# Second stage of a two-stage transformer kernel: order of projections and output columns in the first and the last batch

## The chip, the cores and the metric

The kernel runs on one core of a Trainium2 chip. The metric is the device time of one execution in microseconds (us). A core has five engines that the text names as the profile does: PE (matmuls; PEld is its weight load), DVE (vector), ACT (scalar, which also does the activations), POOL (general purpose) and SP, whose queue (SPq) issues the DMA transfers.

## The reference, cut to what matters

Three stages run one behind the other on 8 batches of 576 tokens and 512 features: a pooled attention, a gated MLP, and a block of four causal attention experts of which each token uses two. Only the last one is touched by the change:

```python
def _moe2_ref(x, w_gate, wq, wk, wv, wo):       # x: 8 x 576 x 512, E = 4 experts, Hd = 64
    logits = x @ w_gate
    topk = np.argpartition(-logits, K, axis=-1)[..., :K]
    ...                                          # w: softmax over the two chosen logits
    for e in range(E):
        q, k, v = x @ wq[e], x @ wk[e], x @ wv[e]
        scores = scale * (q @ k.transpose(0, 2, 1))
        scores = np.where(causal, -1000000000.0, scores)
        a = exp(scores - rowmax); a /= a.sum(-1, keepdims=True) + 1e-09
        ye = a @ v @ wo[e]
        ...                                      # out += w[:, e] * ye where e is chosen
    return out
```

## The kernel before, in words

The class PhaseA computes the first two stages for all batches and leaves their result in DRAM as a high and a low half (a product of two such numbers is taken as three matmuls, high times high, low times high, high times low). The class PhaseB is the experts' stage, and it is what the change touches. The hand-over from PhaseA to PhaseB lies at about 589 us of the span.

PhaseB cuts a batch into two pairs of experts (p = 0, 1) and each pair into nine *units* (table `QT`, L612): unit 0 holds the last 64 queries of both experts, units 1 to 4 are the other four blocks of 128 queries of the first expert from the longest to the shortest, units 5 to 8 those of the second. A unit has three steps:

- `score` (L816): two to six matmuls into PSUM, on DVE the mask with the row maximum (L832, L834, L841), on ACT the exponential with the row sum (L844) into one of five buffers `pr`.
- `scale` (L847): on DVE 1 over the sum (L853 or L855, L856), and the multiplication of the row by it and by the expert's gate (L860). That multiplication runs on POOL, except for the units listed in `SDF` (first batch) and `SDL` (last batch), where it runs on DVE.
- `trans` (L862): transposes on PE (L873, L886), a high half on ACT (L877, L890), a low half on DVE (L882, L891).

Behind unit 5 and unit 8 of a pair follows `av` (L893), the product with v of one expert (PE L906, ACT L910, DVE L911); the second expert's `av` also makes `ah` and `al`, the high and low half of the pair's result (L916 ACT, L917 DVE). They come from four buffers of the tag "x2", so the tiles of one batch can be written only when the output columns of the batch before have read theirs.

Between the units lie the projections, named by short codes. `10` to `13` are q half 0, q half 1, k half 0 and k half 1 of the batch's second pair; `00` to `03` the same of the next batch's first pair; each is 12 matmuls of `proj` (L705, matmuls L713 to L715). Behind q come copies on ACT and subtractions on DVE (L726 to L734) and, after half 1, two DMAs into the tiles `qz` (L737), which the units 1 to 8 need. Behind k come L744 on ACT, L745 on DVE and, after half 1, four DMAs into `kd` (L751). `v0` to `v4` are the v projections (L756: 12 matmuls each, 8 for `v4`), whose last four columns are the gate's logits; `g` is the gate (L789: 13 small DVE steps and one exponential, L796 to L812). `x0` to `x3` load the next batch's input (L634, three DMAs each); its low half `xbl` has a single buffer, so it can be loaded only when all projections of the batch at hand are done. `o0` to `o3` are the output columns of the batch before (`outp`, L919: for each of two query ranges six matmuls, three per pair, then ACT L931; one DMA, L932).

`run` (L934) issues first the list `PRE` (L621) for batch 0, then unit by unit: `score` of unit k, `scale` of unit k-1, the codes that `FIRSTF` (batch 0), `FILL` or `LASTF` (batch 7) list for the unit, `av` where it is due, `trans` of unit k-3. The last batch's own columns come at the end (L977). The framework orders each engine's instructions ahead of the run: by the program's order, but an instruction whose inputs it reckons to be late is overtaken by later ones of the same engine. On the chip each engine then runs its list in order. PSUM has 8 banks, which all tiles of PhaseB share (L702).

Of the kernel before, what the change touches and what calls it, by code (L numbers as in the profile page):

```python
# [8 lines left out]
F32 = mybir.dt.float32  # L9
# [7 lines left out]
B, H, S, D = 8, 8, 576, 64  # L17
# [596 lines left out]
ALV = 1  # L614
KDM = 1
FILL = (('', '12 10 11', '', '13 x0 x1 x2 x3', '', '', 'o3 o1 o0', '', ''), ('v0', 'v1 00 02', '01 o2', '03', '', '', '', 'v2 v3', 'v4 g'))
FIRSTF = (('10', '11', '12', '13 x0 x1 x2 x3', '', '', '', '', ''), ('v0 00', '', '01 02 v1', '03', '', '', '', 'v2 v3', 'v4 g'))
LASTF = (('', '10 12 11', '', '', '13', '', 'o1', '', 'o0'), ('', '', '', '', '', 'o2', '', '', 'o3'))
SDF = {(0, 0), (0, 1), (0, 5), (0, 8), (1, 0), (1, 2), (1, 7)}
SDL = {(0, 4), (0, 6), (1, 6), (1, 7)}  # L620
PRE = 'v0 00 01 02 03 v1 v2 v3 v4 g'  # L621
AVS = [(0, 256), (256, S)]


class PhaseB:


    def __init__(self, ctx, tc, w, ins, x2d, out, ident):
        self.tc, self.nc, self.ins, self.x2d, self.out, self.ident = tc, tc.nc, ins, x2d, out, ident
        self.c = self.w = w  # L630
        self.ps = ctx.enter_context(tc.tile_pool(name="b_ps", bufs=1, space=bass.MemoryType.PSUM))
        self.X, self.QK, self.V, self.GW, self.U, self.PT, self.AV, self.AH = {}, {}, {}, {}, {}, {}, {}, {}

    def load_x(self, b, kc):  # L634
        nc, w = self.nc, self.w
# [211 lines left out]
    def scale(self, b, p, u):  # L847
# [6 lines left out]
        else:  # L854
# [3 lines left out]
        n = min(S, 128 * i + 128)  # L858
        (nc.vector if (p, u) in (SDF if b == 0 else SDL if b + 1 == B else ()) else
         nc.gpsimd).tensor_scalar(pt[:, :n], pt[:, :n], st[:, 3:4], g, op0=OP.mult, op1=OP.mult)  # L860
# [55 lines left out]
            nc.scalar.activation(ah[:, lo:up], a[:, lo:up], AF.Copy)  # L916
            (nc.vector if ALV else nc.gpsimd).tensor_sub(al[:, lo:up], a[:, lo:up], ah[:, lo:up].bitcast(F32))  # L917

    def outp(self, b, f):  # L919
        nc, w = self.nc, self.w  # L920
        c = slice(128 * f, 128 * f + 128)
        o = w.tile([128, S], F32, tag="vg", name="o", bufs=3)
        for lo, up in AVS:
            ps = self.bank("op")[:, :up - lo]
            s = slice(lo, up)
            for p in range(2):
                ah, al = self.AH[b, p]
                nc.tensor.matmul(ps, self.wo[0][:, p, c], ah[:, s], start=p == 0, stop=False)
                nc.tensor.matmul(ps, self.wo[1][:, p, c], ah[:, s], start=False, stop=False)
                nc.tensor.matmul(ps, self.wo[0][:, p, c], al[:, s], start=False, stop=p == 1)  # L930
            nc.scalar.activation(o[:, s], ps, AF.Copy)  # L931
        nc.sync.dma_start(self.out[b, :, f], o)  # L932

    def run(self):  # L934
        self.consts()
        for kc in range(4):
            self.load_x(0, kc)
        self.weights()
        part = lambda b, p: [lambda w=w, h=h: self.proj(b, w, p, h) for w in "qk" for h in range(2)]
        vpart = lambda b: [lambda t=t: self.vproj(b, t) for t in range(NT)]  # L940
        units = [(b, p, u) for b in range(B) for p in range(2) for u in range(9)]
        def item(b, x):
            if x[0] == "x":
                return [lambda: self.load_x(b + 1, int(x[1]))] if b + 1 < B else []
            if x[0] == "o":
                return [lambda: self.outp(b - 1, int(x[1]))] if b > 0 else []
            if x[0] == "1":
                return [part(b, 1)[int(x[1])]]
            if b + 1 == B:
                return []  # L950
            if x[0] == "0":
                return [part(b + 1, 0)[int(x[1])]]
            if x[0] == "v":
                return [vpart(b + 1)[int(x[1])]]
            return [lambda: self.gate(b + 1)]
        for x in PRE.split():
            for f in item(0 if x[0] == "1" else -1, x):
                f()
        for k in range(len(units) + LAG + 1):
            if k < len(units):  # L960
                b, p, u = units[k]
                self.score(b, p, u)
            if 0 <= k - 1 < len(units):
                self.scale(*units[k - 1])
            if k < len(units):
                for x in (LASTF if b + 1 == B else FILL if b else FIRSTF)[p][u].split():
                    for f in item(b, x):
                        f()
            j = k - LAG
            if 0 <= j - 1 < len(units):  # L970
                b_, p_, u_ = units[j - 1]
                if u_ in (5, 8):
                    for g in range(2):
                        self.av(b_, p_, u_ // 8, g)
            if 0 <= j < len(units):
                self.trans(*units[j])
        for f in range(4):  # L977
            self.outp(B - 1, f)


def host_b(inputs, a):
# [34 lines left out]
```

## Time and profile before

| | us |
|---|---|
| median of 3 runs | 968.05 (966.70 to 968.46) |
| the profiled execution | 967.84 |
| its span, first to last instruction | 966.1 |
| PE busy in the span | 915.0 (95%) |
| DVE, ACT, POOL busy | 693.1, 519.0, 447.0 |

The span is what the traces show; the execution's own time is 1.74 us longer than it. A group of instructions is shown with its line, engine, operation, output and inputs. Start times are counted from the span's start. Matmuls overlap, so the length of one is not what it costs; the distance of starts is. A row of busy time by stretch gives the stretch, its length, then the busy us (with the number of instructions) of PE, PEld, DVE, ACT and POOL, the granted clock of PE as a share of 2.4 GHz, the DMA share and GB/s. A row in order of time gives start, length, engine, line and operation, and in brackets the idle time before it with what ended it.

### The profile page before, as it was taken

The page shows a single profiled execution, that of the slowest core. Times are in us where ns is not written, and L with a number is a line of the kernel's source. Part 1 is how long each engine was busy: PE and PEld are TensorE (multiplying, and loading weights), DVE is VectorE, ACT ScalarE, POOL GpSimd, SP SyncE. Part 2 cuts the span into 40 slices and gives each one's busy share as a digit, 9 for nine tenths or more (in the row PEclk, how much of TensorE's full clock was granted, in tenths as well). Part 3 has the DMA queues.
Part 4 walks back from the last instruction along what each step waited for, and adds up shares of the span by engine and source line. Part 5 has one row for each costly group of instructions (what it writes and reads, how often), then busy time and mean ns, then how long its engine had stood idle before and what let it go on. Part 6 is the DMA issues. An engine that isn't in the chain of part 4 may idle for free.

```text
span 966.1 us, 18451 instructions
## 1 busy us (share of the span) xinstructions
PE 915.0 (95%) x6488; PEld 864.4 (89%) x6488; DVE 693.1 (72%) x1869; ACT 519.0 (54%) x1285; POOL 447.0 (46%) x628
## 2 busy tenths in 40 slices
PE   4887699999999999999999999899999999999997
PEld 3677689989989999899899899799999999999987
DVE  6998557757667577577576514897878796878785
ACT  3755334344343343343443433677777777777776
POOL 6545847558369368376583560113222222323221
PEclk9797899999999999999999999999999999999999
DMA  9611522312402404223126014415253534435121
GB/s 326 236 35 44 172 80 82 121 61 71 157 25 81 160 13 140 99 65 132 56 61 191 25 39 134 140 37 176 61 172 88 162 94 147 118 108 163 49 61 75
DMA packets 51644, 102.86 MB, mean 106 GB/s; under 512 B 10592, under 2 KB 16736, under 8 KB 50656
## 3 DMA queue, kind: packets, MB, share of 16 engines
q1 hardware_dynamic: 51408, 101.68, 32.9%
q8 instruction: 52, 0.85, 0.4%
q14 instruction: 40, 0.33, 0.1%
q10 hardware_dynamic: 144, 0.00, 0.0%
HBM read 59.72 MB, written 28.31 MB: 91 GB/s over the span
## 4 chain that ended last, share of the span: by engine, by line
PE 63%; DVE 20%; ACT 6%; POOL 5%; issue 3%; DMA 2%; SPq 1%; POOLq 0%; ACTq 0%; DVEq 0%
PE av L906 4%; PE op L457 4%; PE op L458 4%; PE op L459 3%; PE sp L434 3%; PE sp L432 3%; PE sp L433 3%; PE sc L224 3%; PE t L886 3%; DVE vnl L402 3%; PE pj L715 2%; PE pj L713 2%; PE pj L714 2%; DVE vnh L404 2%; DVE bs L388 2%
## 5 line engine op out<-in xcount | busy, mean ns | idle before, releaser
L860 POOL TENSOR_SCALAR pr<-pr,sm,gw 128x128 f32<-128x128 f32 (+3 forms) x119 | 72.7, 612 | 208.1 <-DVE sm L856 140.9
L844 ACT ACTIVATE pr<-s,sm 128x256 f32<-128x256 f32 (+4 forms) x160 | 83.2, 521 | 41.6 <-DVE sm L841 18.0
L432 PE MATMUL sp<-wsh,vnh 128*128 128x288 f32 x256 | 78.8, 309 | 5.0 <-ACT vnh L400 5.0
L458 PE MATMUL op<-g,woh 128*128 128x288 f32 x256 | 77.0, 301 | 6.8 <-POOL g L445 6.8
L457 PE MATMUL op<-g,woh 128*128 128x288 f32 x256 | 78.5, 309 | 0.3 <-DVE x2l L464 0.3
L416 PE MATMUL up<-x,wih 128*128 128x288 f32 x256 | 76.8, 300 | 1.5 <-ACT xu L324 1.5
L433 PE MATMUL sp<-wsh,vnl 128*128 128x288 f32 x256 | 77.0, 301 | 0.0
L434 PE MATMUL sp<-wsl,vnh 128*128 128x288 f32 x256 | 76.6, 299 | 0.0
L418 PE MATMUL up<-x,wil 128*128 128x288 f32 x256 | 75.7, 296 | 0.0
L715 PE MATMUL pj<-xbh,wql 128*128 128x288 f32 x256 | 75.5, 295 | 0.0
L713 PE MATMUL pj<-xbh,wqh 128*128 128x288 f32 x256 | 75.5, 295 | 0.0
L714 PE MATMUL pj<-xbl,wqh 128*128 128x288 f32 x256 | 75.5, 295 | 0.0
L459 PE MATMUL op<-g,wol 128*128 128x288 f32 x256 | 75.3, 299 | 0.0
L417 PE MATMUL up<-x,wih 128*128 128x288 f32 x256 | 75.1, 293 | 0.0
L841 DVE CUSTOM_DVE_ANT_0 s<-s,mk 128x512 f32<-128x512 f32 (+3 forms) x128 | 62.4, 487 | 3.5 <-PE t L886 2.9
L224 PE MATMUL sc<-kbd,qt 128*128 128x144 f32 (+1 forms) x320 | 50.8, 306 | 14.2 <-DMA qt<-q_in 8.4
L891 DVE TENSOR_TENSOR pbl<-t,pbh 128x512 fp32r<-128x512 f32 (+3 forms) x128 | 60.7, 484 | 3.4 <-ACT pbh L890 1.7
L886 PE MATMUL t<-ident,pr 128*128 128x128 f32 x320 | 57.7, 280 | 4.8 <-POOL pr L860 2.6
L224 PEld LDWEIGHTS sc<-kbd,qt 128*128 128x128 f32 (+1 forms) x320 | 44.4, 192 | 18.3 <-issue 11.1
L906 PE MATMUL av<-pbh,vt 128*128 128x320 f32 (+4 forms) x224 | 55.6, 278 | 2.4 <-ACT pbh L890 2.4
L400 ACT ACTIVATE vnh<-vg,rs 128x512 fp32r<-128x512 f32 (+1 forms) x40 | 27.3, 717 | 54.9 <-POOL rs L392 43.0
L464 POOL TENSOR_TENSOR x2l<-x2l,x2h 128x576 fp32r<-128x576 f32 x8 | 11.4, 1430 | 97.1 <-ACT x2h L463 97.1
(247 smaller groups left out, 3352.8 us busy)
## 6 DMA issues: line engine op xcount, KB each, us to landing
kraw<-k_in SPq DMA_DIRECT2D x16, 576.0 KB, 3.8
x<-x2h SPq DMA_DIRECT2D x32, 288.0 KB, 2.1
x<-x2l SPq DMA_DIRECT2D x32, 288.0 KB, 2.1
xbl<-x SPq DMA_DIRECT2D x32, 288.0 KB, 4.1
xbh<-x SPq DMA_DIRECT2D x32, 288.0 KB, 4.0
kd<-scr SPq DMA_DIRECT2D x64, 144.0 KB, 2.5
out<-o SPq DMA_DIRECT2D x32, 288.0 KB, 3.7
vraw<-v_in SPq DMA_DIRECT2D x16, 512.0 KB, 4.3
```

What stands on the lines that cost most here:

```text
L224: nc.tensor.matmul(ps[:m, p // 2, (p % 2) * 144:(p % 2) * 144 + 144], qt[:, p, o:o + m], kbd[:, p, :], start=p % 2 == 0, stop=True, skip_g ...
L432: nc.tensor.matmul(o, vh[:, k, c], self.ws[0][:, k, s], start=k == 0, stop=False)
L433: nc.tensor.matmul(o, vl[:, k, c], self.ws[0][:, k, s], start=False, stop=False)
L434: nc.tensor.matmul(o, vh[:, k, c], self.ws[1][:, k, s], start=False, stop=False)
L457: nc.tensor.matmul(o, self.wo[0][:, k, c], gh[:, s], start=k == 0, stop=False)
L458: nc.tensor.matmul(o, self.wo[0][:, k, c], gl[:, s], start=False, stop=False)
L459: nc.tensor.matmul(o, self.wo[1][:, k, c], gh[:, s], start=False, stop=k == 3)
L713: nc.tensor.matmul(ps, self.wq[0][:, kc, c], xh[:, s], start=kc == 0, stop=False)
L714: nc.tensor.matmul(ps, self.wq[0][:, kc, c], xl[:, s], start=False, stop=False)
L715: nc.tensor.matmul(ps, self.wq[1][:, kc, c], xh[:, s], start=False, stop=kc == 3)
L886: nc.tensor.transpose(ps[:, j], pt[:, 128 * j:128 * j + 128], self.ident)
L906: nc.tensor.matmul(ps[:, s - lo:], vt[:, j, 2 * p + e].rearrange("p a d -> p (a d)"), t[:, e, j * PTS + s:j * PTS + up], start=j == 0 and ...
```

## The change

The list `PRE` now starts with the k projections, then come the v projections and the gate, and the q projections last. In the first batch `12` comes ahead of `11`, and `11` and `13` (with the loads of the next input) come one unit later; the next batch's `v0 00` move from unit 0 to unit 1 of the second pair, and `01 02 v1` are reordered. `SDF` keeps two of its seven entries: five scalings go from DVE to POOL. In the last batch `11` moves from unit 1 to unit 3, and the previous batch's columns `o2` and `o3` move from units 5 and 8 of the second pair to units 0 and 3. The last batch's columns 0 and 1 are begun by halves: the three matmuls per range that need the first pair only are issued behind the last unit (`TAILF`), and their PSUM banks are held until the second pair's result is there. The very last column is sent in two DMAs, one per range.

```diff
--- before.py
+++ after.py
@@ -614,11 +614,12 @@
 ALV = 1
 KDM = 1
 FILL = (('', '12 10 11', '', '13 x0 x1 x2 x3', '', '', 'o3 o1 o0', '', ''), ('v0', 'v1 00 02', '01 o2', '03', '', '', '', 'v2 v3', 'v4 g'))
-FIRSTF = (('10', '11', '12', '13 x0 x1 x2 x3', '', '', '', '', ''), ('v0 00', '', '01 02 v1', '03', '', '', '', 'v2 v3', 'v4 g'))
-LASTF = (('', '10 12 11', '', '', '13', '', 'o1', '', 'o0'), ('', '', '', '', '', 'o2', '', '', 'o3'))
-SDF = {(0, 0), (0, 1), (0, 5), (0, 8), (1, 0), (1, 2), (1, 7)}
+FIRSTF = (('10', '12', '11', '', '13 x0 x1 x2 x3', '', '', '', ''), ('', 'v0 00', 'v1 02 01', '03', '', '', '', 'v2 v3', 'v4 g'))
+LASTF = (('', '10 12', '', '11', '13', '', 'o1', '', 'o0'), ('o2', '', '', 'o3', '', '', '', '', ''))
+TAILF = ('i0', '', '', 'i1')
+SDF = {(0, 0), (0, 1)}
 SDL = {(0, 4), (0, 6), (1, 6), (1, 7)}
-PRE = 'v0 00 01 02 03 v1 v2 v3 v4 g'
+PRE = '02 03 v0 v1 v2 v3 v4 g 00 01'
 AVS = [(0, 256), (256, S)]
 
 
@@ -629,7 +630,7 @@
         self.tc, self.nc, self.ins, self.x2d, self.out, self.ident = tc, tc.nc, ins, x2d, out, ident
         self.c = self.w = w
         self.ps = ctx.enter_context(tc.tile_pool(name="b_ps", bufs=1, space=bass.MemoryType.PSUM))
-        self.X, self.QK, self.V, self.GW, self.U, self.PT, self.AV, self.AH = {}, {}, {}, {}, {}, {}, {}, {}
+        self.X, self.QK, self.V, self.GW, self.U, self.PT, self.AV, self.AH, self.OP = {}, {}, {}, {}, {}, {}, {}, {}, {}
 
     def load_x(self, b, kc):
         nc, w = self.nc, self.w
@@ -916,20 +917,29 @@
             nc.scalar.activation(ah[:, lo:up], a[:, lo:up], AF.Copy)
             (nc.vector if ALV else nc.gpsimd).tensor_sub(al[:, lo:up], a[:, lo:up], ah[:, lo:up].bitcast(F32))
 
-    def outp(self, b, f):
+    def outp(self, b, f, pair=None):
         nc, w = self.nc, self.w
         c = slice(128 * f, 128 * f + 128)
-        o = w.tile([128, S], F32, tag="vg", name="o", bufs=3)
-        for lo, up in AVS:
-            ps = self.bank("op")[:, :up - lo]
+        first = pair == 0
+        o = None if first else w.tile([128, S], F32, tag="vg", name="o", bufs=3)
+        last = (b, f) == (B - 1, 3)
+        for i, (lo, up) in enumerate(AVS):
+            if first or pair is None:
+                self.OP[f, i] = self.bank("op")[:, :up - lo]
+            ps = self.OP[f, i]
             s = slice(lo, up)
-            for p in range(2):
+            for p in range(2) if pair is None else (pair,):
                 ah, al = self.AH[b, p]
                 nc.tensor.matmul(ps, self.wo[0][:, p, c], ah[:, s], start=p == 0, stop=False)
                 nc.tensor.matmul(ps, self.wo[1][:, p, c], ah[:, s], start=False, stop=False)
                 nc.tensor.matmul(ps, self.wo[0][:, p, c], al[:, s], start=False, stop=p == 1)
+            if first:
+                continue
             nc.scalar.activation(o[:, s], ps, AF.Copy)
-        nc.sync.dma_start(self.out[b, :, f], o)
+            if last:
+                nc.sync.dma_start(self.out[b, :, f, s], o[:, s])
+        if not first and not last:
+            nc.sync.dma_start(self.out[b, :, f], o)
 
     def run(self):
         self.consts()
@@ -966,6 +976,9 @@
                 for x in (LASTF if b + 1 == B else FILL if b else FIRSTF)[p][u].split():
                     for f in item(b, x):
                         f()
+            else:
+                for x in TAILF[k - len(units)].split():
+                    self.outp(B - 1, int(x[1]), 0)
             j = k - LAG
             if 0 <= j - 1 < len(units):
                 b_, p_, u_ = units[j - 1]
@@ -975,7 +988,7 @@
             if 0 <= j < len(units):
                 self.trans(*units[j])
         for f in range(4):
-            self.outp(B - 1, f)
+            self.outp(B - 1, f, 1 if f < 2 else None)
 
 
 def host_b(inputs, a):
```

## Rows read from the trace of the kernel before

**Rows 1.** The page's 40 slices: PE's busy tenths.

```profile
PE   4887699999999999999999999899999999999997
```

**Rows 2.** Busy time by stretch, first batch.

```profile
601.00:604.20 3.20, 3.20 (x28) 3.20 (x27) 1.35 (x6) 1.16 (x4) 0.00 (x0) 1.00 0.27 61
604.20:611.00 6.80, 6.80 (x51) 6.67 (x50) 6.38 (x31) 6.09 (x17) 0.73 (x1) 1.00 0.12 27
611.00:620.30 9.30, 4.95 (x31) 3.61 (x30) 8.47 (x38) 5.89 (x19) 1.98 (x4) 0.95 0.91 250
620.30:622.70 2.40, 2.40 (x12) 2.40 (x12) 1.19 (x4) 0.95 (x3) 0.91 (x2) 0.50 0.95 338
```

**Rows 3.** PE in order of time, first batch: start, length, line; in brackets the wait.

```profile
594.24 0.29 PE L715 MATMUL pj<-xbh,wql 128*128 128x288 f32 x1
...
603.09 0.30 PE L713 MATMUL pj<-xbh,wqh 128*128 128x288 f32 x1
...
603.36 0.31 PE L828 MATMUL s<-kd,qs 128*128 128x320 f32 x1
...
619.62 1.09 PE L886 MATMUL t<-ident,pr 128*128 128x128 f32 x4 [1.45 <-DVE sm L855]
...
621.95 0.42 PE L781 MATMUL vp<-wqh,xbh 128*128 128x260 f32 x1
```

**Rows 4.** DVE in order of time: q's last subtraction, the gate's first and last step.

```profile
595.98 0.53 DVE L731 TENSOR_TENSOR qs<-pj,qs 64x224 fp32r<-64x224 f32 x2
...
605.17 0.17 DVE L796 TENSOR_REDUCE gs<-lg 128x5 f32<-128x20 f32 x1
...
609.14 0.34 DVE L812 COPY wl<-gw 64x2 f32<-64x2 f32 x2
```

**Rows 5.** ACT in order of time: the table load and the exponential behind it.

```profile
604.73 1.28 ACT L844 ACT_TABLE_LOAD   x1
606.02 0.53 ACT L844 ACTIVATE pr<-s,sm 128x320 f32<-128x320 f32 x1
```

**Rows 6.** The scaling of unit 8 (128 wide) on DVE, another, 512 wide, on POOL.

```profile
623.39 0.35 DVE L860 TENSOR_SCALAR pr<-pr,sm,gw 128x128 f32<-128x128 f32 x1
...
631.53 0.78 POOL L860 TENSOR_SCALAR pr<-pr,sm,gw 128x512 f32<-128x512 f32 x1 [10.33 <-DVE sm L856]
```

**Rows 7.** Groups by line and shape, DVE, 601.0 to 620.3 us: the scaling of 512.

```profile
L860 DVE TENSOR_SCALAR pr<-pr,sm,gw 128x512 f32<-128x512 f32 x2 | 1.1, 540 | 0.0
```

**Rows 8.** SP's queue in order of time: the last load of the second batch's input.

```profile
619.75 0.43 SPq L644 DMA_DIRECT2D xbh<-x  x1
```

**Rows 9.** DMA issues: KB each, us from issue to landing (588 to 625; 940 to 967).

```profile
qzvhi<-qs SPq DMA_DIRECT2D x1, 128.0 KB, 2.3
...
out<-o SPq DMA_DIRECT2D x6, 288.0 KB, 2.1
```

**Rows 10.** Busy time by stretch, last batch (columns as in rows 2).

```profile
940.00:955.60 15.60, 13.26 (x99) 12.48 (x99) 13.75 (x53) 12.26 (x39) 4.11 (x7) 1.00 0.10 39
955.60:962.50 6.90, 6.82 (x50) 6.34 (x49) 1.75 (x4) 4.23 (x11) 0.00 (x0) 1.00 0.27 102
```

**Rows 11.** PE in order of time, last batch: first av, o2, o3, the last columns.

```profile
936.02 0.28 PE L906 MATMUL av<-pbh,vt 128*128 128x256 f32 x1
...
944.55 0.28 PE L928 MATMUL op<-ah,wqh 128*128 128x256 f32 x1
...
946.16 0.49 PE L886 MATMUL t<-ident,pr 128*128 128x128 f32 x3
...
948.49 0.33 PE L928 MATMUL op<-ah,wqh 128*128 128x256 f32 x1
...
955.56 0.36 PE L928 MATMUL op<-ah,wqh 128*128 128x256 f32 x1
```

**Rows 12.** ACT and DVE, last batch: ah of the first pair, al of the second.

```profile
950.18 0.78 ACT L916 ACTIVATE ah<-scr 128x256 fp32r<-128x256 f32 x2
...
956.77 0.97 DVE L917 TENSOR_TENSOR al<-scr,ah 128x256 fp32r<-128x256 f32 x2
```

## What the change should do to the time, predicted from these rows

> **What bounds the kernel now.** I went from the page's slices to the stretches, then to each engine in order of time, then to transfers. The slices [rows 1] show PE at nine tenths or more from the seventh slice on, except in slice 26 (603.8 to 628.0 us) and in the last. So PE is the bound in the middle batches, which the change leaves alone. What can be had lies where PE is not full: the first and the last batch of the second stage.
>
> *First batch.* PE is full up to 611.0 and busy only 4.95 of 9.30 us from there to 620.3: 4.35 us idle, while DVE is busy 8.47 of the 9.30 [rows 2]. Then it runs at half clock, 1.2 GHz, for 2.40 us [rows 2]. The reader is to see that PE ran ahead with the projections 10 to 13 and then had nothing but units, each of which waits for DVE; the longest wait, 1.45 us, is unit 5's transposes standing for DVE [rows 3], which has to do that unit's scaling first. DVE's backlog begins at 604.2 (6.38 of 6.80 us busy from there), because the gate, from 605.17 to 609.48 [rows 4], falls on top of the first scores; just before, from 601.0 to 604.2, DVE was busy only 1.35 of 3.20 us [rows 2]. PE gets other work only when the second batch's input is there: its last load is issued at 619.75 [rows 8], v0 starts at 621.95 [rows 3].
>
> *Last batch.* From 940.0 to 955.6 PE is busy 13.26 us, 2.34 idle, DVE 13.75 [rows 10]. Behind it the four last columns keep PE busy alone, from 955.56 to the end of PE's work, about 6.9 us [rows 10, 11].
>
> The profiled execution took 967.84 us, 0.21 below the median of 968.05; the sum is made against 967.84 and 0.2 is added at the end.
>
> **The change part by part.**
>
> 1. *PRE: k and the gate first, q last.* Nothing is added. The gate (13 DVE steps and one exponential) moves from 605.17 into the DVE gap before 604.2: 3.20 - 1.35 = 1.85 us of DVE time were free there [rows 2]. Against it, q's copies and subtractions now come last, and unit 0 needs them. From about 601.2 on (v4's end, unmoved) DVE then has the gate (4.3 us with two scores between [rows 4], estimated 3 without) and q's subtractions (0.53 for the last two [rows 4], estimated 1.9 for all), so unit 0's scores can start near 606; before, they lay around 603.36 [rows 3]. PE is covered by 10, 12 and 11, 12 matmuls of about 0.13 us each, 4.8 us: the order already lets a projection overtake a score (L713 stands ahead of L828 [rows 3]). Gain: DVE starts its backlog earlier by at least the wait for v4's copy, at most by the gap, so between 0 and 1.85 us; a loss is a rival below. I take 1.2, nearer to the gap because gate and q together fill it. If the cover is gone, PE waits from q's last matmul to the last q row in `qz`: copies and subtractions end 2 us later (596.51 [rows 4] for a q that ended at 594.53 [rows 3]), the DMA lands 2.3 us after its issue [rows 9], some 3.3 us in all, estimated, as the subtractions and the DMA overlap. On SP's queue the four kd transfers now go ahead of the two qz transfers; kd is out about 7 us before q ends, so they don't meet. POOL's one step of v4 moves up with it, POOL being idle there (0.73 us busy in 6.80 [rows 2]).
>
> 2. *The exponential's table load* (1.28 us on ACT) now falls to the gate's exponential, between q's two halves, instead of to unit 0's [rows 5]. The row shows the next exponential starting 0.01 us after the load ends, so the load costs 1.28 us on ACT wherever it stands, and that is in the 606 above: 0 in the sum.
>
> 3. *Five scalings from DVE to POOL.* On DVE a scaling of 512 takes 0.54 [rows 7], of 128 takes 0.35 [rows 6]; units 5 and 8 of the first pair, which lie in the DVE-bound stretch, free 0.89 us. The other three lie where PE is full: 0. On POOL the 512 takes 0.78 [rows 6], 0.24 longer, and POOL has room (1.98 us in 9.30 [rows 2]). Gain between -0.24 and 0.89; I take 0.9, because the wait before unit 5's transposes is a wait for DVE's turn, longer than POOL's extra.
>
> 4. *The half clock.* 2.40 us at 0.50 cost 1.2 us of work, behind 4.35 us of idling [rows 2]. If idling halves, the clock may hold or not: 0 to 1.2, I take 0.6.
>
> 5. *11, 13 and the loads one unit later, v0 00 too.* 13's end opens `xbl`; from 13's end (611.0) to v0 pass 10.9 us of kd and twelve loads on SP's queue [rows 3, 8]. As PE is full until 611 either way, 13 should end at about the same time: 0, with up to 2.7 lost if it ends later (rival A). The move of v0 to unit 1 lets two units go to DVE before the heap of projections: 0 to some tenths, taken as 0.
>
> 6. *Last batch, 11, o2, o3 earlier.* A column is 12 matmuls in 1.61 us (944.55 to 946.16 [rows 11]). o2 now comes ahead of the `av` at 936.02, and pushes `av` and the next transposes back by up to 1.61 us; in return 3.2 us of PE work leave the stretch behind 944.55. o3 earlier frees the "x2" tiles: `ah` of the first pair was written at 950.18, right behind o3 (948.49 to 950.13) [rows 11, 12], late for halves to be begun. 0, between -1.6 and +1.0.
>
> 7. *Columns 0 and 1 by halves.* 12 of the last 48 matmuls, 12 x 0.134 = 1.6 us, leave the stretch behind 955.56 for one with 2.34 us idle [rows 10]. The wait for `al` (956.77 to 957.74 [rows 12]) is still covered by 12 first-pair matmuls of columns 2 and 3. With the four held banks, those two columns need the other four. Gain 1.6, between 0.5 (banks or cover short) and 2.1 (the 0.5 of stall in the 6.9 us also goes: 6.9 - 48 x 0.134).
>
> 8. *The last column in two transfers.* One more issue on SP, ahead of the end. Landing takes 2.1 us for 288 KB and 2.3 for 128 KB [rows 9]: size doesn't show, so 0, between 0 and 0.3. By "DMA: Bandwidth & Descriptors" of the Trainium skill (the path's two cost components, a fixed 2.0 us plus bytes over 436e9 per second) 128 KB less would be an estimated 0.3 us less; the two rows don't bear it out, and the sum by it would be 4.6 instead of 4.3.
>
> Sum: 1.2 + 0.9 + 0.6 + 1.6 = **4.3 us** saved: 967.84 - 4.3 + 0.2 = 963.7.
>
> **The rivals.**
>
> A. *The input is late.* 13 and its loads slip by 2.7 us; PE idles for the input and the start wins nothing. For it: the loads take 10.9 us of queue behind 13. Against: 13 is ready early and can overtake. 967.84 - 1.6 + 0.2 = 966.4.
>
> B. *Slower: PE stands at q.* If 10, 12 and 11 are not ordered ahead of units 0 and 1, PE idles 3.3 us behind PRE and falls to half clock as it did after 4.35 us of idling, 1.2 more, and 13 and the input slip as much, so that nothing at the start makes it good: 967.84 + 4.5 - 1.6 + 0.2 = 970.9. It decides from 3.5 us lost on. Against: rows 3.
>
> C. *The end wins nothing.* o2 ahead of `av` delays the units by 1.6 us, as much as the halves save: 967.84 - 2.7 + 0.2 = 965.3. For it: DVE is as full as PE behind 940 [rows 10].
>
> D. *Nothing changes.* The order of issue was already moved by the framework, so the engines run nearly the same lists: 968.0. Against: the gate can't overtake v4.
>
> E. *The table load drains ACT.* ACT then stands 1.38 us longer between q's halves, and term 1 becomes -0.2: 965.1. Against: the 0.01 us behind the load [rows 5]. "ScalarE: Activation LUTs" of the Trainium skill (What ACT_TABLE_LOAD costs) gives 1283 ns plus a drain of 1380 ns per switch of sets; this trace agrees with the first and shows no second.
>
> **How the numbers follow.** About 0.2% (1.9 us) is what a measurement of this kernel can tell from no change: faster ends at 966.1, slower begins at 970.0. Chances: forecast 0.48 (its own range 961.5 to 965.5), A 0.17, B 0.10, C 0.14, D 0.08, E 0.03. Faster: 0.48 + 0.14 + 0.03 and a little under a third of A, 0.05: 0.70. Slower: B, 0.10. Same: the rest, 0.20. The range's low end takes the upper bounds of terms 1 and 4 and part of term 7's (about 7 us saved), 960.9; its high end, 968.2, takes in A, C, D, E and leaves out B.
>
> **What would show it.** Right: DVE busy with the gate before 604.2; unit 0's first score near 606 with PE full before it; idle between 611 and 622 near 2 us, and little or no half clock; two first-pair column halves ahead of the last `av`, and 36 matmuls, some 5 us, behind it. Wrong: a PE wait of over 2 us around 603; v0 of the second batch later than 623 with PE idle before it; L906 of the first pair in the last batch behind o2 with DVE idle; the last columns still 6.9 us long.

## The result, and the profile after

The changed kernel is **slower**: 976.35 us (975.52 to 978.85, six runs) against 968.91 for the kernel before on the same chip (966.70 to 971.03, six runs), ratio 1.008, 95% interval 1.0066 to 1.0095. Forecast were 963.7 and a range up to 968.2. The six executions of the kernel before differ by 4.3 us among themselves, so medians, not single times, are compared.

The profiled execution took 975.52 us with a span of 973.7, 7.6 longer than before. Line numbers behind L618 are one to thirteen higher than before (L713 is L714, L860 is L861, L928 to L930 are L933 to L935, L931 is L938); of the experiments, those that change only lists of the kernel before keep its numbers. The page's slices of PE, which answer to [rows 1], show little: slice 25 (584.2 to 608.6 us) falls from nine tenths to eight, the last one from seven to six.

```profile
PE   4887699999999999999999998899999999999996
```

A split of the span finds the loss. Two marks lie in every kernel of this study: the first PE instruction of the experts' stage, and the last batch's `v4`, whose last matmul is where its group of instructions ends ("first to last start"). The two groups, of before and of after:

```profile
L767 PE MATMUL vp<-wqh,xbh x32: 281/283/335, 601.9 to 914.1; 128*128 128x260 f32 x32
```

```profile
L768 PE MATMUL vp<-wqh,xbh x32: 281/284/335, 597.9 to 916.4; 128*128 128x260 f32 x32
```

With the stage's start at 589.70 before and 588.88 after, the **main part** (stage start to last `v4`) took 324.4 us and takes 327.5, 3.1 more; the **end** (from there to the end of the span) took 52.0 and takes 57.3, 5.3 more. Both parts lose, and the first stage, which the change leaves alone, happened to be 0.8 shorter: 3.1 + 5.3 - 0.8 = 7.6.

*The first batch.* Busy time by stretch, to be read beside [rows 2]:

```profile
601.00:604.90 3.90, 1.20 (x10) 0.97 (x8) 3.29 (x11) 2.83 (x7) 0.68 (x1) 1.00 0.07 17
604.90:608.30 3.40, 3.31 (x14) 3.34 (x15) 1.42 (x6) 0.44 (x2) 0.00 (x0) 0.51 0.25 57
617.30:621.70 4.40, 1.19 (x8) 0.83 (x8) 3.95 (x18) 3.02 (x11) 1.77 (x3) 1.00 0.92 268
621.70:625.40 3.70, 3.70 (x17) 3.70 (x18) 2.10 (x12) 1.55 (x6) 1.62 (x3) 0.55 1.02 324
```

Where PE was full before 604, it is now idle for 2.70 of 3.90 us and then runs 3.4 us near half clock (0.51); behind the old gap, which is still there, the half clock lasts 3.70 us instead of 2.40. PE in order of time, beside [rows 3]:

```profile
601.91 0.29 PE L716 MATMUL pj<-xbh,wql 128*128 128x288 f32 x1
604.99 0.82 PE L828 MATMUL s<-kd,qs 128*128 128x320 f32 x2 [2.79 <-issue]
605.61 0.44 PE L714 MATMUL pj<-xbh,wqh 128*128 128x288 f32 x1
...
618.57 0.44 PE L887 MATMUL t<-ident,pr 128*128 128x128 f32 x2 [1.26 <-POOL pr L861]
...
620.26 0.33 PE L887 MATMUL t<-ident,pr 128*128 128x128 f32 x1 [1.02 <-POOL pr L861]
...
621.70 0.81 PE L887 MATMUL t<-ident,pr 128*128 128x128 f32 x4 [0.94 <-POOL pr L861]
...
626.98 0.28 PE L782 MATMUL vp<-wqh,xbh 128*128 128x260 f32 x1
```

The first row is q's last matmul, the second the first two matmuls of unit 0's score, the third the projection `10`. The score stands ahead of the projection in PE's list, and everything behind it waits for q. It stood there in the kernel before, too, where q had long been ready; this row of PE comes ahead of the L713 and the L828 that [rows 3] shows:

```profile
602.82 0.43 PE L827 MATMUL s<-kd,qs 128*128 128x320 f32 x2
```

So only the score's later matmuls (L828) had been overtaken. What q waits for stands on DVE and ACT, in order of time:

```profile
600.53 0.17 DVE L797 TENSOR_REDUCE gs<-lg 128x5 f32<-128x20 f32 x1
...
604.44 0.45 DVE L730 TENSOR_TENSOR qs<-pj,qs 64x288 fp32r<-64x288 f32 x1
...
605.54 0.34 DVE L813 COPY wl<-gw 64x2 f32<-64x2 f32 x2
```

```profile
601.07 1.28 ACT L799 ACT_TABLE_LOAD   x1
602.37 0.22 ACT L799 ACTIVATE gg<-gg 128x20 f32<-128x20 f32 x1
...
603.04 0.40 ACT L727 ACTIVATE qs<-pj 64x288 fp32r<-64x288 f32 x1
```

The gate did move into DVE's gap (600.53 to 605.9, before 605.17 to 609.48 [rows 4]). But q's half 1, done on PE at 602.20, is copied only at 603.04, behind the table load, the gate's exponential and half 0, and its first subtraction ends at 604.89; 0.10 us later PE goes on.

*The last batch.* Busy time by stretch, beside [rows 10], and PE's waits, beside [rows 11]:

```profile
940.00:951.50 11.50, 10.76 (x80) 9.91 (x79) 8.67 (x31) 8.62 (x28) 3.14 (x5) 1.00 0.20 77
951.50:957.80 6.30, 2.70 (x15) 2.36 (x16) 5.64 (x26) 3.96 (x13) 1.22 (x2) 0.90 0.01 3
957.80:960.00 2.20, 2.20 (x11) 2.20 (x11) 0.97 (x3) 0.38 (x1) 0.45 (x1) 0.50 0.00 0
```

```profile
927.42 0.39 PE L907 MATMUL av<-pbl,vt 128*128 128x256 f32 x1 [1.14 <-DVE pbl L892]
...
954.68 0.33 PE L887 MATMUL t<-ident,pr 128*128 128x128 f32 x1 [2.81 <-POOL pr L861]
```

Before 951.5 DVE is now idle for 2.8 of 11.5 us; behind it PE is idle for 3.6 of 6.3 us, and a half clock follows that the end did not have before. The chain that releases the long wait is on DVE and POOL (the 2.81 us are put down to POOL, which itself waited for DVE's 1 over the sum):

```profile
953.31 0.15 DVE L856 TENSOR_SCALAR sm<-sm 128x1 f32<-128x1 f32 x1
...
953.84 0.16 DVE L857 RECIPROCAL sm<-sm 128x1 f32<-128x1 f32 x1
```

```profile
954.17 0.45 POOL L861 TENSOR_SCALAR pr<-pr,sm,gw 128x128 f32<-128x128 f32 x1 [4.86 <-DVE sm L857]
```

Before, `o2` and `o3` lay around the same transposes (unit 4's, at 948.14 there): `o2` ended at 946.16, two units' transposes ahead of them, and `o3` began at 948.49, right behind them [rows 11].

### The profile page after: what moved, and what is told of

It is laid out like the page before. It is cut to its first block, busy times and chain, and to the rows that moved or that the text cites. A ratio compares the mean times of both kernels' runs of the same rounds, so it can differ in the third digit from the quotient of the medians.

```text
span 973.7 us, 18457 instructions
## 1 busy us (share of the span) xinstructions
PE 917.0 (94%) x6488; PEld 866.0 (89%) x6488; DVE 692.7 (71%) x1864; ACT 517.5 (53%) x1285; POOL 449.3 (46%) x633
## 4 chain that ended last, share of the span: by engine, by line
PE 63%; DVE 20%; ACT 6%; POOL 5%; issue 3%; DMA 2%; SPq 1%; ACTq 0%; POOLq 0%; DVEq 0%
PE av L907 4%; PE op L457 4%; PE op L458 3%; PE op L459 3%; PE sp L434 3%; PE sp L433 3%; PE sp L432 3%; PE sc L224 3%; PE t L887 3%; DVE vnl L402 3%; PE pj L714 3%; PE pj L716 2%; PE pj L715 2%; DVE vnh L404 2%; DVE bs L388 2%
## 5 line engine op out<-in xcount | busy, mean ns | idle before, releaser
L861 POOL TENSOR_SCALAR pr<-pr,sm,gw 128x128 f32<-128x128 f32 (+2 forms) x123 | 74.6, 608 | 209.9 <-DVE sm L857 160.6
L714 PE MATMUL pj<-xbh,wqh 128*128 128x288 f32 x256 | 76.0, 297 | 0.9 <-issue 0.9
L887 PE MATMUL t<-ident,pr 128*128 128x128 f32 x320 | 57.4, 278 | 6.8 <-POOL pr L861 6.8
```

Of the source, the lines that this page charges most:

```text
L714: nc.tensor.matmul(ps, self.wq[0][:, kc, c], xh[:, s], start=kc == 0, stop=False)
L887: nc.tensor.transpose(ps[:, j], pt[:, 128 * j:128 * j + 128], self.ident)
```

## The experiments

All ratios are to the kernel before on the same chip, with the 95% interval; main part and end are of the profiled execution. Kernels whose first batch is as before have main parts of 323.7 to 325.4 (in one, with other scalings only, 326.1), so a main part is good to about 1 us; kernels whose end is as before have ends of 51.9 to 52.0, so an end is good to 0.1. One execution of each kernel was profiled, and it need not be a typical one.

| run | ratio | main part | end |
|---|---|---|---|
| before | | 324.4 | 52.0 |
| the change | 1.0080 (1.0066 to 1.0095) | 327.5 | 57.3 |
| e1_start | 1.0042 (1.0027 to 1.0057) | 326.8 | 51.9 |
| e7_pre | 1.0028 (1.0015 to 1.0041) | 327.9 | 52.0 |
| e4_sdf | 1.0001 (0.9988 to 1.0013) | 326.1 | 52.0 |
| e14_firstf | 1.0002 (0.9990 to 1.0015) | 324.6 | 52.0 |
| e3_cover | 1.0017 (1.0002 to 1.0032) | 323.3 | 52.0 |
| e12_cover_sdf | 1.0010 (0.9999 to 1.0020) | 324.6 | 52.0 |
| e15_cover3_split | 1.0005 (0.9992 to 1.0017) | 325.2 | 51.6 |
| e2_end | 1.0066 (1.0049 to 1.0084) | 325.1 | 57.4 |
| e5_early | 1.0052 (1.0033 to 1.0071) | 325.3 | 56.5 |
| e9_o2 | 1.0033 (1.0022 to 1.0043) | 323.8 | 55.8 |
| e10_o3 | 1.0019 (1.0004 to 1.0035) | 324.3 | 53.9 |
| e11_11 | 1.0008 (0.9997 to 1.0018) | 324.6 | 53.1 |
| e6_halves | 0.9994 (0.9984 to 1.0004) | 325.4 | 52.5 |
| e13_otile | 1.0001 (0.9991 to 1.0011) | 323.7 | 52.0 |

**e1_start and e2_end: the two ends of the change apart.** e1_start is the kernel before with three lists of the change, e2_end the change with these three lists as before.

```diff
-PRE = 'v0 00 01 02 03 v1 v2 v3 v4 g'
+PRE = '02 03 v0 v1 v2 v3 v4 g 00 01'
-FIRSTF = (('10', '11', '12', '13 x0 x1 x2 x3', '', '', '', '', ''), ('v0 00', '', '01 02 v1', '03', '', '', '', 'v2 v3', 'v4 g'))
+FIRSTF = (('10', '12', '11', '', '13 x0 x1 x2 x3', '', '', '', ''), ('', 'v0 00', 'v1 02 01', '03', '', '', '', 'v2 v3', 'v4 g'))
-SDF = {(0, 0), (0, 1), (0, 5), (0, 8), (1, 0), (1, 2), (1, 7)}
+SDF = {(0, 0), (0, 1)}
```

> Kernel before with the change's first batch alone (PRE, FIRSTF, SDF). The traces put v4 of the last batch (L767/L768) 2.3 us later after the change although the second stage began 0.8 us earlier, so the first batch should have cost 3.1 us. Theory (the start and the end are two losses that add): this kernel is 2 to 4 us slower than before, PE stands 2.8 us ahead of unit 0's first score and then runs at half clock for some 3 us. Rival (the whole loss sits in the last batch and the start only shifts idling about): within 1 us of before.

> Changed kernel with the first batch of before, so the change's last batch alone. Theory: 4.5 to 6 us slower than before, with a PE wait of 2.8 us for a scaling of the second pair's unit 4 and half clock behind it. Rival (the tail goes wrong only because it is entered late or in another rhythm): less than 2 us slower.

Measured: 1.0042 and 1.0066, by the medians 3.8 and 6.2 us. Each loses by itself, as both theories have it (e2_end by 0.2 us more than its range), and the two losses (0.0042 + 0.0066 = 0.0108) add up to the change's 0.0080 or somewhat more, within the intervals. In the profile the end's loss is the same with either start (57.4 and 57.3).

**e7_pre, e4_sdf, e14_firstf: the three lists of the start, one at a time.** Each takes one of the three line pairs above.

> Only PRE of the change (k and the gate first, q last); FIRSTF, SDF and the last batch as before. Theory (the loss at the start is PE standing for q behind PRE, with the half clock after it, because unit 0's score stands ahead of the projection 10 in PE's list): the PE wait of about 2.8 us ahead of unit 0's score is here too, with half clock behind it, and the time is 2 to 4 us over the kernel before, ratio 1.002 to 1.004, little less than with all three edits of the start (1.0042). Rival (the loss comes from the five scalings moved to POOL, whose steps PE waited for at 619.9, 621.6 and 623.1 in that run): with the scalings on DVE those waits are gone and the ratio is within 0.999 to 1.001, though PE stands once for q.

> Only SDF of the change: five scalings of the first batch go from DVE to POOL, everything else as before. Theory (a scaling's start is set by the reciprocal ahead of it on DVE, so a POOL scaling that takes longer only ends later, and DVE's free time is not where PE waits): no gain, ratio 0.9995 to 1.0015; the 1.45 us wait of unit 5's transposes for DVE becomes a wait for POOL of about the same length or longer. Rival (the prediction's term): DVE is relieved in the stretch that it bounds, 0.9 us faster, ratio 0.9985 to 0.9995, and the idle of PE between 611 and 620 falls below 3.8 us.

> Only FIRSTF of the change: 12 ahead of 11, the projections 11 and 13 with the next input's loads one unit later, v0 and 00 one unit later; PRE, SDF and the last batch as before. Theory (these projections and the input come later, so PE has less to do among the first units, but the input is there before PE runs dry): ratio 0.9995 to 1.0010; the last input load is issued 1 to 3 us later than at 619.75. Rival (the later input holds PE, as the prediction's rival A has it): the last load is issued 3 us or more later, v0 of the second batch starts behind 624 with PE idle before it, and the ratio is 1.0015 to 1.003, which is what the three edits of the start cost beyond PRE alone.

The order of PRE alone costs 1.0028; the other two cost nothing that can be measured alone. e7_pre has the same wait and the same half clock as the change (PE in time, then busy time by stretch):

```profile
607.85 0.50 PE L827 MATMUL s<-kd,qs 128*128 128x320 f32 x2 [2.79 <-issue]
```

```profile
607.80:611.20 3.40, 3.34 (x14) 3.05 (x15) 1.54 (x7) 0.43 (x2) 0.00 (x0) 0.59 0.22 51
```

In e4_sdf the wait ahead of unit 5's transposes, 1.45 us for DVE before [rows 3], is 1.53 us for POOL:

```profile
620.93 1.09 PE L886 MATMUL t<-ident,pr 128*128 128x128 f32 x4 [1.53 <-POOL pr L860]
```

PE is idle for 3.51 of the 9 us from 611 to 620 there, below the 3.8 that the rival named, but only because this stage starts 1.2 us later (590.92) and the wait ends at 620.93; over the same part of the stage, 612.2 to 621.5, PE idles for 4.4 us, as before. The ratio is the theory's: what DVE was relieved of did not reach PE. In e14_firstf the last input load, issued at 619.75 before [rows 8], comes at 623.08 (SP's queue in time), and PE waits for the input once:

```profile
623.08 0.43 SPq L644 DMA_DIRECT2D xbh<-x  x1
```

```profile
626.78 0.39 PE L781 MATMUL vp<-wqh,xbh 128*128 128x260 f32 x1 [0.28 <-DMA xbh<-x]
```

Counted from the stage's start that is 2.4 us later (32.5 against 30.1), and it costs 0.3 us of waiting. Whether the three lists together cost more than PRE alone (1.0042 against 1.0028) stays open, as the intervals overlap.

**e3_cover, e12_cover_sdf, e15_cover3_split: is there a gain once PE is covered?** The first projections of the second pair are put at the end of PRE, so that they stand ahead of unit 0's score. e3_cover is e1_start with

```diff
-PRE = '02 03 v0 v1 v2 v3 v4 g 00 01'
+PRE = '02 03 v0 v1 v2 v3 v4 g 00 01 10 12'
-FIRSTF = (('10', '12', '11', '', '13 x0 x1 x2 x3', '', '', '', ''), ...
+FIRSTF = (('', '', '11', '', '13 x0 x1 x2 x3', '', '', '', ''), ...
```

> e1_start with 10 and 12 put into PRE behind q, so that 24 matmuls (3.2 us) stand ahead of unit 0's first score whatever the framework reckons. Theory (the start's loss is the missing cover, with the half clock it brings): PE's wait near 605 goes, no half clock there, and the kernel is 3 to 5 us faster than e1_start, 0 to 2 us faster than before. Rival (DVE's backlog sets the pace and PE's wait only moves): PE's idle time moves behind 611, and the kernel is within 1 us of e1_start.

e12_cover_sdf is the same with SDF of before:

> The start of the change with the projections 10 and 12 added to the end of PRE, and SDF as before (the seven scalings on DVE); the last batch as before. Theory: with PE covered behind q, the start gains nothing with five scalings on POOL because unit 5's transposes then wait for POOL (2.79 us at 620.3 in the run with cover and SDF of the change); with SDF of before this wait shrinks to under 1 us and the time falls by 1 to 2 us against that run (ratio 1.0017), to 0.999 to 1.001. Rival (the heap of DVE work is the bound there, whoever scales): a wait for DVE of 2 us or more takes its place and the ratio stays at 1.001 to 1.003.

e15_cover3_split is the kernel before with this, and with the last column in two transfers:

```diff
-PRE = 'v0 00 01 02 03 v1 v2 v3 v4 g'
+PRE = '02 03 v0 v1 v2 v3 v4 g 00 01 10 11 12'
-FIRSTF = (('10', '11', '12', '13 x0 x1 x2 x3', '', '', '', '', ''), ...
+FIRSTF = (('', '', '', '13 x0 x1 x2 x3', '', '', '', '', ''), ...
...
+            if (b, f) == (B - 1, 3):
+                nc.sync.dma_start(self.out[b, :, f, s], o[:, s])
+        if (b, f) != (B - 1, 3):
+            nc.sync.dma_start(self.out[b, :, f], o)
```

> k and the gate first as in the change, but the projections 10, 11 and 12 stand behind q at the end of PRE, 13 and the loads stay where they were, the scalings as before; in the last batch only the very last column goes in two transfers, nothing is moved and nothing is begun by halves. From the start of the second stage to v4 of the last batch the kernel before takes 324.4 us, from there to the end 52.0. Theory (the gate's gain exists, but only while PE is covered for all of q's way through DVE): PE does not wait for q (under 0.5 us), no half clock behind it, and the first part takes 322.5 to 324; the split last column saves 0.3 to 0.5 of the 52.0; ratio 0.997 to 0.9995. Rival (the gate first only shifts DVE's backlog behind q's subtractions and those of the three projections): a wait of 2 us or more for DVE stands ahead of unit 0's or unit 1's transposes, the first part takes 324.5 or more, ratio 1.000 to 1.002.

Measured: 1.0017, 1.0010, 1.0005. The cover takes more than half of the loss back and wins nothing: e3_cover is 1.8 us faster than e1_start and still 2.0 slower than before, outside the ranges of its theory and of its rival. PE's waits in e3_cover:

```profile
606.92 0.39 PE L828 MATMUL s<-kd,qs 128*128 128x320 f32 x1 [0.82 <-issue]
...
612.61 0.74 PE L873 MATMUL t<-ident,pr 128*128 128x128 f32 x5 [1.83 <-DVE sm L856]
...
620.29 0.66 PE L886 MATMUL t<-ident,pr 128*128 128x128 f32 x4 [2.79 <-POOL pr L860]
```

and in e15_cover3_split, where the first of the three is gone:

```profile
614.17 0.74 PE L873 MATMUL t<-ident,pr 128*128 128x128 f32 x5 [2.93 <-DVE sm L855]
```

The wait moves from q to unit 0's transposes, which waited 0.23 us in the kernel before, and grows with the cover: of e15_cover3_split's two accounts the rival came true. Unit 0 itself is late. Its first step on DVE in the kernel before, then the end of its score on PE and that first step in e3_cover and in e15_cover3_split:

```profile
604.18 0.42 DVE L832 CUSTOM_DVE_ANT_1 s<-s,mk 128x256 f32<-128x256 f32 x1
```

```profile
607.86 0.28 PE L829 MATMUL s<-qs 128*128 128x256 f32 x1
608.18 0.43 DVE L832 CUSTOM_DVE_ANT_1 s<-s,mk 128x256 f32<-128x256 f32 x1
```

```profile
608.33 0.28 PE L829 MATMUL s<-qs 128*128 128x256 f32 x1
609.88 0.42 DVE L832 CUSTOM_DVE_ANT_1 s<-s,mk 128x256 f32<-128x256 f32 x1
```

With the stage's starts at 589.70, 589.47 and 589.73, unit 0's first step on DVE is 4.2 and 5.7 us later than before. Most of that is PE's order: the score now stands behind q and behind 24 or 36 covering matmuls, and ends 4.3 and 4.5 us later (in the kernel before it ended at 604.05). In e3_cover DVE takes it up 0.04 us behind its end; in e15_cover3_split another 1.27 us pass in which DVE is still at the subtractions of the covering projections. By the program PE's list is no shorter in another order: what brings `v4` and the gate forward puts q, and with it unit 0, back. An order with the gate early and q not last was not tried. e12_cover_sdf turns the wait of 2.79 us for POOL into one of 2.27 for DVE ahead of the same transposes, as its rival has it, and its ratio lies where both allow it. e3_cover's 323.3 is the shortest main part of the study, in an execution without a half clock from 601 to 628, and this execution (966.6 us) is the fastest of twelve with a median of 970.7.

**e5_early, e9_o2, e10_o3, e11_11: the moves of the last batch.** All leave the halves away (`TAILF` empty, whole columns at the end) and keep the split of the last column. e5_early has the change's `LASTF`; the three others keep back part of it, in this order:

```diff
-LASTF = (('', '10 12 11', '', '', '13', '', 'o1', '', 'o0'), ('', '', '', '', '', 'o2', '', '', 'o3'))
+LASTF = (('', '10 12', '', '11', '13', '', 'o1', '', 'o0'), ('o2', '', '', '', '', '', '', '', 'o3'))
+LASTF = (('', '10 12', '', '11', '13', '', 'o1', '', 'o0'), ('', '', '', 'o3', '', 'o2', '', '', ''))
+LASTF = (('', '10 12', '', '11', '13', '', 'o1', '', 'o0'), ('', '', '', '', '', 'o2', '', '', 'o3'))
```

> e2_end without the halves: o2, o3 and 11 moved as in the change, the last four columns whole at the end (the last one in two transfers). Theory (the loss comes from o2 and o3 moved ahead: the stretch behind them starves DVE first and PE afterwards): as slow as e2_end or slower, 4 to 7 us over before, and the long wait for unit 4's scaling is there without any half column. Rival (the halves, which stand in PE's list or hold four PSUM banks, make the waits): within 1.5 us of before.

> e5_early with o3 back at unit 8, so o2 and 11 alone are moved, no halves. Theory A (o2 ahead of av and the transposes delays what DVE waits for, and its place is empty later): 54 us or more from v4 to the end, DVE idle between unit 0 and unit 3 of the second pair. Theory B (o3 does it, by freeing the tiles for ah and al early, so that four more steps stand ahead of the scalings in DVE's list): 51 to 53 us.

> e5_early with o2 back at unit 5, so o3 and 11 alone are moved, no halves. Theory A (o2 does it): 51 to 53.5 us from v4 to the end. Theory B (o3 does it, through ah and al ahead of the scalings on DVE): 54 us or more, and PE's wait of 2.8 us for unit 4's scaling is there.

> e5_early with o2 and o3 back at units 5 and 8, so 11 alone is moved (and the last column goes in two transfers). The changed kernel's trace shows a wait of 1.14 us for DVE behind 11, ahead of the first pair's first av, where before had 0.65 and 0.34. Theory (11 is a small part): 51.5 to 53 us from v4 to the end. Rival (11 starts it, since its subtractions then fall between unit 3 and unit 4 on DVE and everything behind comes late): 54 us or more.

The ends add up. The split alone gives 51.6 (e15_cover3_split). `11` two units later: 53.1, so 1.5 lost. `o2` besides: 55.8, 2.7 more. `o3` instead: 53.9, 0.8 more. All three: 56.5, against 51.6 + 1.5 + 2.7 + 0.8 = 56.6. e5_early has its theory's loss (4.9 us by the medians, though 1.4 less than e2_end) and its long wait without any half column (2.82 us for POOL), and e9_o2 came out as its Theory A has it. e10_o3's 53.9 lies between its two ranges and e11_11's 53.1 just above its theory's, and by the ratios e11_11 can't be told from the kernel before; these two shares rest on the profiles.

PE's idle time in the end, summed, is 7.0 us in e15_cover3_split, 8.1 in e11_11, 8.4 in e10_o3, 9.3 in e9_o2 and 10.1 in e5_early. So `11` costs 1.1 us of waiting, a little at each of several places. The first is the last `av` of the batch before (not the first pair's, as the expectation says), ahead of which `11` now stands; it waits 1.14 us, in the kernel before 0.65 and 0.34. In e11_11, then in the kernel before:

```profile
925.19 0.39 PE L907 MATMUL av<-pbl,vt 128*128 128x256 f32 x1 [1.14 <-DVE pbl L892]
...
942.11 0.53 PE L907 MATMUL av<-pbh,vt 128*128 128x256 f32 x2 [1.37 <-ACT pbh L891]
```

```profile
924.47 0.53 PE L906 MATMUL av<-pbh,vt 128*128 128x256 f32 x2 [0.65 <-ACT pbh L890]
...
926.31 0.39 PE L906 MATMUL av<-pbl,vt 128*128 128x256 f32 x1 [0.34 <-DVE pbl L891]
```

`o2`'s loss is the wait at unit 4's transposes, ahead of which it had been cover (the kernel before, then e9_o2), and then a lower clock: 0.66 granted from 950 to 954, in the last of these fences, where e6_halves and the kernel before have 1.00.

```profile
948.14 0.33 PE L886 MATMUL t<-ident,pr 128*128 128x128 f32 x1 [0.69 <-POOL pr L860]
```

```profile
950.83 0.33 PE L887 MATMUL t<-ident,pr 128*128 128x128 f32 x1 [2.56 <-POOL pr L861]
```

```profile
950.00:954.00 4.00, 3.17 (x15) 3.18 (x16) 2.95 (x16) 2.46 (x10) 1.22 (x2) 0.66 0.02 4
```

The wait is 1.87 us longer, about the 1.61 of the column that no longer stands ahead of it. In its new place the column gives some of that back (the `av` at 942.56 waits 0.43 us, in e11_11 1.37), so 1.1 us of idling are left; the low clock takes 1.7 us of work more, and the two make the 2.7. `o3`'s 0.8 isn't explained by waits, which grow by 0.2 us only.

**e6_halves and e13_otile: the halves without the moves.** e6_halves is e2_end with `LASTF` of before; e13_otile besides gives the last column's output a tile that no transfer reads:

```diff
-        o = None if first else w.tile([128, S], F32, tag="vg", name="o", bufs=3)
+        o = None if first else w.tile([128, S], F32, tag="raw" if last else "vg", name="o", bufs=3)
```

> e2_end with LASTF of before: o2, o3 and 11 stay where they were, columns 0 and 1 are begun by halves, the last one goes in two transfers. Measured by the time from v4's last matmuls in the last batch (L767, L768) to the end of the span: 52.0 us before, 57.3 changed, 56.5 without the halves (e5_early). Theory (the loss is the move of o2 and o3): 51 to 53 us, and the run within 2 us of before. Rival (the halves alone disturb the order as well): 55 us or more.

> Columns 0 and 1 by halves and the last column in two transfers, with the previous batch's columns and the projection 11 where they were before, and the last column's output tile in another tag, so that it does not wait for the first column's transfer. Theory (the halves' gain is taken back by two things, 1.6 us of halves ahead of the last av, and the last column's copy standing 0.8 us for a tile that a transfer still reads): against the run with the old tile (0.9994) it is 0.6 to 0.9 us faster, ratio 0.9983 to 0.9988; the last ACT copy starts right behind the last matmul. Rival (the transfer of the last column is limited elsewhere, in SP's queue or in the DMA engines behind the other three columns): the copies come earlier but the end does not, ratio 0.9990 to 1.0000.

Measured: 0.9994 and 1.0001, ends of 52.5 and 52.0. Against the split alone (51.6) the halves lose 0.9, and 0.9 is also what they add to the moves (e2_end 57.4, e5_early 56.5). PE in e6_halves shows the first half of a begun column, at 951.05, ahead of the last `av`, which ends at 957.2 (the other half begins at 954.28); the first whole column behind that `av` starts at 957.03, before at 955.56 [rows 11]:

```profile
951.05 0.39 PE L933 MATMUL op<-ah,wqh 128*128 128x256 f32 x1
...
957.03 0.36 PE L933 MATMUL op<-ah,wqh 128*128 128x256 f32 x1
```

Counted from `v4` (914.5 here, 914.1 before) that is 1.1 us later, and the columns then take 5.9 us instead of 7.0: PE's work ends 48.4 us behind `v4` in both.

The four columns now finish so close together that the fourth needs a buffer which the first column's transfer still reads (ACT in e6_halves, PE having ended at 962.95):

```profile
963.44 0.71 ACT L938 ACTIVATE o<-op 128x256 f32<-128x256 f32 x2 [1.48 <-DMA out<-o]
```

The other tile takes that wait away, but the last transfers then take longer to land. DMA issues with KB and us from issue to landing, in e13_otile (in e15_cover3_split, whose columns are spread out, both take 1.8):

```profile
out<-o SPq DMA_DIRECT2D x1, 160.0 KB, 2.2
out<-o SPq DMA_DIRECT2D x1, 128.0 KB, 2.6
```

Of the 0.6 to 0.9 us expected, 0.5 came in the profile (52.5 to 52.0) and none that the medians could tell; the rival, a limit in the transfers, is right in part. No version of this study beats the kernel before by more than a measurement can tell; the split column is the only part with a visible gain, 0.4 us in the profile's end; no run has it by itself.

## Why the prediction was wrong

*Term 1, "PE is covered by 10, 12 and 11": failed.* The step was read from too few rows: that L713 stands ahead of L828 [rows 3] is no overtaking of the score, whose first matmuls, L827, stand ahead of that L713 (602.82 above). The framework kept that order, unit 0's score ahead of `10`, and PE stood 2.79 us, estimated as 3.3 in rival B. That is rival B's mechanism, to which 0.10 was given; e7_pre shows it alone and e3_cover leaves 0.82 us of it. Of the 1.2 us gained nothing is left even with cover (e15_cover3_split): "DVE starts its backlog earlier" counted the gate's time as saved and not that unit 0's first step on DVE comes 4 us or more later. The 606 for unit 0's score was about right (604.99), but it was not asked what that costs against 602.82. *Term 5, 0 for `11`, `13` and the loads:* held by itself (e14_firstf, 1.0002).

*Term 2, the table load:* no drain, as [rows 5] had it: the next exponential starts 0.02 us behind the load. But its 1.28 us now lie on q's way, ahead of the copy at 603.04; what that costs by itself was not tried.

*Term 3, the scalings: 0.9 forecast, 0 measured* (e4_sdf, 1.0001). Unit 5's wait changed its releaser, not its length.

*Term 4, the half clock: wrong sign.* There are two stretches now, 3.40 us at 0.51 and 3.70 at 0.55, which cost 3.40 x 0.49 + 3.70 x 0.45 = 3.3 us of work, against 1.2 before. With PE's waits (2.79 + 1.26 + 1.02 + 0.94 = 6.0, before 4.35) the stretch loses 3.8 us, near the 3.1 of the main part.

*Rival A, the late input:* the input was late. Counted from the stage's start the last load is issued 5.0 us later in the change than before. SP's queue:

```profile
623.96 0.43 SPq L645 DMA_DIRECT2D xbh<-x  x1
```

But no wait stands ahead of `v0` at 626.98 above: PE got there no sooner than the input, so no row charges the loss to it.

*Term 6, `11`, `o2` and `o3`: the largest error.* Taken as 0, bounded at -1.6; measured -1.5, -2.7 and -0.8, together -5.0 (e5_early, 56.5 against 51.6, has them as -4.9). The bound counted the delay of `av` by one column. What it left out is that PE's work taken from a stretch leaves a hole there when that stretch is paced by DVE and POOL: of the "3.2 us of PE work" that leave it, counted as room for the units, `o2` was the cover of a wait, which grew from 0.69 to 2.56 us (e9_o2), and the clock fell behind it. The place of that cover was in the rows shown [rows 11].

*Term 7, the halves: +1.6 forecast, -0.9 measured.* The 1.6 us do leave the stretch behind the last `av` (the whole columns take 5.9 us in the change, 963.8 to 969.7, forecast some 5, before 7.0 [rows 10, 11]). They are paid ahead of it: "2.34 us idle" was a sum over 15.6 us, and in e6_halves the whole columns start 1.1 us later and PE ends no sooner. Then the fourth output tile waits 1.48 us.

*Term 8, the split column: 0 forecast, 0.4 measured* (51.6 against 52.0). From the last matmul's end to the end of the span pass 3.58 us before and 3.12 in e15_cover3_split; the half lands in 1.8 us, the whole column in 2.1. The two rows of [rows 9] were of different transfers, a `qz` write beside an output, and so no test of size. The Trainium skill, "DMA: Bandwidth & Descriptors" (the path's two cost components), whose figures are for transfers issued by GpSimd, would have an estimated 0.3 us for 128 KB less. The runs on SP's queue, 0.3 between the two landings and 0.4 at the end, agree with that better than with the 0 taken.

*The sum.* Forecast +4.3. Measured: main part -3.1 (good to about 1), end -1.5 - 2.7 - 0.8 - 0.9 + 0.4 = -5.5, in the profile -5.3. Rival C had the end's mechanism half right, `o2` ahead of `av` delaying the units, but only as much as the halves save; no case had the end lose. The range's low end does not follow from what it names: the upper bounds of terms 1, 4 and 7 with term 3's 0.9 make 1.85 + 1.2 + 2.1 + 0.9 = 6.05 us, not 7; the measured time lies beyond its other end.

## What to carry to other kernels

Before work is moved out of a stretch, look at which wait stands right behind it: if another engine ends that wait, the work was its cover, and the move costs what that wait grows by, less what the work covers in its new place, and more where the clock falls. A sum of idle time over a long stretch is not room; room is idle time at the place in the engine's list where the new work will stand, and only there. And an order read from a few rows has to be read from the group's first instruction on: name the instruction that will stand first in the new list and price the case in which it blocks.

## What was not expected of the hardware

A small step of the gate, L802 with two SBUF inputs of 80 elements, took 0.66 us instead of 0.24 (the same step, L801, at 605.89 before); it starts while POOL subtracts v4's low half, and ends 0.10 us after POOL's step does (DVE, then POOL, in time, of the change):

```profile
601.12 0.66 DVE L802 TENSOR_TENSOR ga<-ga,tri 128x80 f32<-128x80 f32 x1
```

```profile
600.83 0.85 POOL L776 TENSOR_TENSOR vt<-vs,vt 128x256 fp32r<-128x256 f32 x1 [9.83 <-ACT vt L775]
```

In e3_cover it is the same step (0.66, POOL 0.85 instead of 0.73); in e12_cover_sdf it is the step ahead of it, 0.80 instead of 0.23. Both end 0.10 to 0.11 us behind POOL's. The Trainium skill, "SBUF — State Buffer" (SBUF: two separate sides), has DVE and GpSimd share a pair of ports, which a DVE step with two SBUF inputs and a GpSimd step that reads SBUF hold in turn, the other one blocked; these traces agree. In the kernel before a step of the gate meets POOL's too: L799 takes 0.37 us, its like, L800, 0.23; it ends 0.10 us behind POOL's step, which runs from 604.79 to 605.52:

```profile
605.25 0.37 DVE L799 TENSOR_TENSOR ga<-lg 128x80 f32<-128x80 f32 x1
```

So it costs 0.4 us in the change, 0.14 before.
